# A delta-rule recurrence feeding a SwiGLU layer on one core: the first chunk's chain in another order, and the lower words of the weights added by DMA

## The chip, the cores and the metric

The kernel runs on one core of a Trainium2 chip. The metric is the device time of one execution in microseconds; the kernel before takes 877.96 us (median of 17 runs).

## The reference

Two layers follow each other. The first is a delta-rule recurrence per batch and head, over 768 steps with a 48 x 48 state; the second is a feed-forward layer with an RMS norm in front.

```python
B, H, S, D = (4, 8, 768, 48)
k_n = k / (norm(k, axis=-1) + 1e-06)
for t in range(S):
    y[:, :, t] = einsum('bhd,bhde->bhe', q[:, :, t], state)
    v_old = einsum('bhde,bhd->bhe', state, k_n[:, :, t])
    state = state + beta_t * einsum('bhd,bhe->bhde', k_n[:, :, t], v[:, :, t] - v_old)
x = y as (B*S, H*D)                       # 3072 x 384
xn = x / sqrt(mean(x*x) + 1e-06) * rms_g
out = (silu(xn @ w_gate) * (xn @ w_val)) @ w_out   # d_ff 1536
```

q, k, v and beta arrive as 32-bit floats. The three weight matrices arrive as 64-bit floats and are read as two 32-bit words per number.

## The kernel before

**Chunks and units.** The 768 steps are cut into 6 chunks of 128; a chunk of one batch (8 heads) is a unit. Within a chunk the recurrence is solved as a triangular system: the inverse of a unit triangular matrix of 128 x 128 per head, in blocks of 32 (W). `invert` computes the inverses of the 32 x 32 diagonal blocks of all 32 heads at once on VectorE, with heads and blocks on the partitions: 31 steps of two operations (L440, L449). To get from the layout of the score matrices to that layout, `gather` writes blocks to a DRAM buffer (gd, L359) and reads them back (gblk, L364). The inverses come back the same way: ttb to DRAM (td, L457), then 16 small loads into tt (L468). The same inverses, transposed and multiplied by minus beta (L459), go to DRAM as nd (L473) and come back as ne in 8 loads (L475).

**The chain of a unit** (`recur`): `corner` makes an off-diagonal 32-block of the inverse from two products, p_v with tt (L509) and p_w with ne (L516), copied out by ScalarE (vs, L524; tt, L526). `inner` then forms p_z, p_x and u from the values, `outer` the output p_y and its norm (ScalarE square L718, GpSimd power L727), and `transpose_y` scales y on ScalarE (L731) and transposes it into xt, the input of the feed-forward layer. For the first chunk units 0 and 1 are written out by hand (L637 to L666), the two interleaved with `stay_warm(n)`, which issues n idle matmuls, with `convert(n)`, which issues n steps of the weight conversion, and with `mask_queries`.

**Weights** (`weights`, L230). 18 tiles of 128 x 768 numbers (6 of each half of gate and value, 3 of each half of out: order gate, value, out for the first half, then for the second). A tile is fetched into raw (three buffers, `fetch`, L212), the first three fetches from SP's queue and the others from GpSimd's. ScalarE makes top from the higher word (`shrink`, L225; two buffers); VectorE then takes five steps: shift (L235), sign (L244), exponent part into the weight (L256), times the lower word (L260), plus top (L265). A new fetch follows the fourth step. The top of tile i+1 is issued just before step three of tile i.

**Order.** `begin` writes out the order of everything up to the end of the first inverse: norms of the keys (`normalize`: square on ScalarE L285, sum on VectorE L287, maximum L290 and power L291 on GpSimd, then scaling L294 to L296), their transposes, the key scores, and, during the inverse, queries' transposes and scores. After that a plan of generators with due times sets the order: the feed-forward layer (`ffn`) advances three units per 128 of d_ff, the conversion's remaining steps are due every 0.6 units, and chunks 1 to 5 run beside it. Each engine works through its instructions in that order; where a tile has no free buffer, the instruction that writes it waits for the last reader of an earlier one.

```python
CYC = 3 * FT * B // 2
for i, m in enumerate((0, 1, 0, 1)):
    at(CYC // 4 * i, ffn(m, half_f * (i // 2), half_f * (i // 2 + 1)))
at(0, convert_rest(0.6))
at(1, first)
...
with tc.manual_schedule():
    begin()
    next(first)
    run_plan(60)
run_plan()
```

Of the kernel before, what the change touches and what calls it, by code (L numbers as in the profile page):

```python
# [10 lines left out]
FP32 = mybir.dt.float32  # L11
# [3 lines left out]
ALU = mybir.AluOpType  # L15
# [12 lines left out]
def kernel(  # L28
# [177 lines left out]
    def fetch():  # L206
        i = len(raws)
        if i < len(todo):
            raw = bits.tile([128, WT], I64, name="raw", bufs=3)
            src = todo[i][1]  # L210
            to = raw if len(src.shape) == 2 else raw.rearrange("p (n m) -> p n m", m=DM)
            (nc.sync if i < 3 else nc.gpsimd).dma_start(out=to, in_=src)  # L212
            raws.append(raw)

    def words(raw):
# [14 lines left out]
    def weights():  # L230
        for i, ((dst, src), raw) in enumerate(zip(todo, raws)):
            low, high = words(raw)
            top = tops[i]
            top_u, dst_u = top.bitcast(U32), dst.bitcast(U32)
            nc.vector.tensor_scalar(  # L235
                out=top_u,
                in0=top_u,
                scalar1=3,
                scalar2=0x7FFFFFFF,
                op0=ALU.logical_shift_left,  # L240
                op1=ALU.bitwise_and,
            )
            yield
            nc.vector.scalar_tensor_tensor(  # L244
                out=top_u,
                in0=high,
                scalar=0x80000000,
                in1=top_u,
                op0=ALU.bitwise_and,
                op1=ALU.bitwise_or,  # L250
            )
            yield
            if i + 1 < len(todo):
                tops.append(shrink(raws[i + 1]))

            nc.vector.tensor_scalar(  # L256
                out=dst_u, in0=top_u, scalar1=0xFF800000, scalar2=None, op0=ALU.bitwise_and
            )
            yield
            nc.vector.scalar_tensor_tensor(  # L260
                out=dst, in0=low, scalar=2.0**-52, in1=dst, op0=ALU.mult, op1=ALU.mult
            )
            fetch()
            yield
            nc.vector.tensor_tensor(out=dst, in0=dst, in1=top, op=ALU.add)  # L265
            yield
        bits_pool.close()

# [13 lines left out]
    def normalize(n):  # L282
        kn = kpad[n % NK]
        ksq = work.tile([128, H, D], FP32, name="ksq", bufs=1)
        nc.scalar.square(ksq, kn[:, :, 0:D])  # L285
        ksum = work.tile([128, H], FP32, name="ksum")
        nc.vector.tensor_reduce(out=ksum, in_=ksq, axis=AXL.X, op=ALU.add)  # L287
        knrm = work.tile([128, H], FP32, name="knrm")

        nc.gpsimd.tensor_scalar_max(ksum, ksum, 1e-30)  # L290
        nc.gpsimd.tensor_tensor(out=knrm, in0=ksum, in1=half, op=ALU.pow)  # L291
        yield
        krec = work.tile([128, H], FP32, name="krec")
        nc.vector.tensor_scalar_add(knrm, knrm, 1e-6)  # L294
        nc.vector.reciprocal(krec, knrm)
        (nc.vector if n < B else nc.gpsimd).tensor_tensor(  # L296
            out=kn[:, :, 0:D],
            in0=kn[:, :, 0:D],
            in1=krec[:, :, None].to_broadcast([128, H, D]),
            op=ALU.mult,  # L300
        )
        yield
# [68 lines left out]
    def prepare(n):  # L371
        norm_k = normalize(n)
        next(norm_k)
        yield 1.5
        next(norm_k)
        yield 2.5
        transpose(n, qpad[n % 2], Q0)
        if n + 2 < NU:
            load_q(n + 2)
        yield 3  # L380
        transpose(n, kpad[n % NK], K0)
        yield 2
        score(n, crossed((0, slice(0, 3)), (1, slice(1, 4))), both)
        yield 1
        gather(n)
# [45 lines left out]
    def invert(c, dt):  # L431
        nc.gpsimd.memset(ttb, 0.0)  # L432
        nc.gpsimd.memset(ttb.rearrange("p j i -> p (j i)")[:, 0 : W * W : W + 1], 1.0)
        yield dt
        for i in range(W - 1):
            n = W - 1 - i
            shape = [128, i + 1, n]
            tmp_b = work.tile([128, W * W // 4], FP32, name="tmp")
            tmp = tmp_b[:, 0 : n * (i + 1)].rearrange("p (k j) -> p k j", j=n)
            nc.vector.scalar_tensor_tensor(  # L440
                out=tmp,
                in0=gblk[:, i, None, i + 1 :].to_broadcast(shape),
                scalar=nbeta[:, c, i : i + 1],
                in1=ttb[:, 0 : i + 1, i : i + 1].to_broadcast(shape),
                op0=ALU.mult,
                op1=ALU.mult,
            )
            to = ttb[:, 0 : i + 1, i + 1 :]
            nc.vector.tensor_tensor(out=to, in0=to, in1=tmp, op=ALU.add)  # L449
            if c == 0 and i > W // 2:  # L450
                stay_warm(2, tmp_b[:, 0 : min(128, n * (i + 1))])
            yield dt
        if c == 0:
            stay_warm(20)
        td = dram.tile([128, W, W], FP32, name="td")
        nd = dram.tile([128, W, W], FP32, name="nd")
        nc.sync.dma_start(out=td, in_=ttb)  # L457

        nc.vector.tensor_tensor(  # L459
            out=gblk,  # L460
            in0=ttb.rearrange("p s m -> p m s"),
            in1=nbeta[:, c, :, None].to_broadcast([128, W, W]),
            op=ALU.mult,
        )
        for b in range(B):
            for a in (1, 3, 0, 2):
                o = W * (a % 2)
                nc.sync.dma_start(  # L468
                    out=tt[b][W * a : W * (a + 1), :, o : o + W],
                    in_=td[a * BH + b * H : a * BH + (b + 1) * H].rearrange("h r j -> r h j"),  # L470
                )
            if b == 0:
                nc.sync.dma_start(out=nd, in_=gblk)  # L473
            for a in (0, 2):
                nc.sync.dma_start(  # L475
                    out=ne[W * a : W * (a + 1), b * H : (b + 1) * H],
                    in_=nd[a * BH + b * H : a * BH + (b + 1) * H].rearrange("h r j -> r h j"),
                )
        yield dt
# [13 lines left out]
    def recur(c, dt):  # L493
# [4 lines left out]
            return beta_t[p, c, b * H : (b + 1) * H, None].to_broadcast([HC, H, D])  # L498


        def corner(b_v, b_w):
            p_v = ps_delta([128, H, W], "p_v") if b_v in units else None
            p_w = ps_delta([128, H, W], "p_w") if b_w in units else None
            for h in range(H):
                for a in (0, 2):
                    wa, wb = (slice(W * x, W * (x + 1)) for x in (a, a + 1))
# [7 lines left out]
                        )  # L514
                    if b_w in units:
                        nc.tensor.matmul(  # L516
                            p_w[wa, h], ne[wa, b_w * H + h], vss[b_w][wa, h], skip_group_check=True
                        )
            if b_v in units:
                vss[b_v] = work.tile([128, H, W], FP32, name="vs")  # L520
            for a in (0, 2):
                wa = slice(W * a, W * (a + 1))
                if b_v in units:
                    nc.scalar.copy(vss[b_v][wa], p_v[wa])  # L524
                if b_w in units:
                    nc.scalar.copy(tt[b_w][wa, :, W:HC], p_w[wa])  # L526


        def outer(b_k, b_y):
# [107 lines left out]
        if c == 0:  # L637

            corner(0, None)
            stay_warm(3)  # L640
            convert(1)
            corner(None, 0)
            stay_warm(2)
            corner(1, None)
            inner(None, None, 0)
            convert(1)
            corner(None, 1)
            stay_warm(3)
            inner(0, None, 1)
            stay_warm(4)  # L650
            convert(1)
            inner(1, 0, None)
            stay_warm(4)
            u_0, u_1 = us[0], us[1]
            outer(None, 0)
            mask_queries(1)
            inner(None, 1, None)
            stay_warm(2)
            convert(1)
            outer(None, 1)  # L660
            convert(1)
            transpose_y(0, scale(*ys.pop(0)))
            stay_warm(4)
            convert(2)
            transpose_y(1, scale(*ys.pop(1)))
            convert(4)  # L666
            yield
# [34 lines left out]
        for s in range(-3, B + 2):  # L702
# [1 line left out]
            yield dt  # L704
            outer(s + 1, s - 1)
            yield dt
            corner(s + 3, s + 2)
            if s - 1 in units:
                ys[s - 1] = scale(*ys[s - 1])
            if s - 2 in units:  # L710
# [108 lines left out]
    def begin():  # L819
        setup()  # L820
        stay_warm(14)
        norms = [normalize(n) for n in range(B)]
        for n in range(3):
            next(norms[n])
        next(norms[0])
        transpose(0, kpad[0], K0)
        next(norms[3])
        tops.append(shrink(raws[0]))
        next(norms[1])
        transpose(1, kpad[1], K0)  # L830
        for n in range(B):
            p_gs = score_part(n, K0)
# [7 lines left out]
        for i in range(W):  # L840
# [5 lines left out]
                load_v(n)  # L846
            if what == 3 and n < B:
                keep_queries(n, score_part(n, Q0))
            if i == 6:
                nc.scalar.memzero(tt_all)  # L850
            if i == 12:
# [61 lines left out]
```

## Time and profile before

| what | us |
|---|---|
| median of 17 runs | 877.96 (876.89 to 882.01) |
| profiled execution | 881.04 |
| its span | 879.3 |
| TensorE busy | 826.8 |
| VectorE busy | 409.9 |
| ScalarE busy | 252.5 |
| GpSimd busy | 106.5 |

The profile counts an engine as busy while an instruction runs; matmuls are pipelined, so a busy TensorE is not one at its peak. In the lists that follow, L and a number is the line of the code, a name with an arrow is what is written and read, and what stands in square brackets is the idle time ahead of an instruction and what ended it. DMA issues are shown by the engine whose queue they are on (SPq, ACTq, POOL). Of the span, the first 95 us lie before the first product of the feed-forward layer; from 95 to about 180 the weight conversion runs beside it; the second chunk's inverse ends at 209.5.

### The profile page before, as it was taken

To read this page: it belongs to the slowest core of one execution; us is meant where nothing else is said; L and a number is where in the kernel's file an instruction comes from. 1 tells how busy PE (TensorE), PEld (TensorE's weight loads), DVE (VectorE), ACT (ScalarE), POOL (GpSimd) and SP (SyncE) were. 2 spreads that over 40 slices of the span, in tenths; PEclk is the share of its full clock that TensorE was granted. 3 is DMA by queue.
4 is the path that set the end of the run, shared out by engine and by line. 5 is a ranking of instruction groups with operands and counts; after the bars stand their busy time and mean duration, and the time that the engine had idled before them with its cause. 6 is when DMAs were issued, how large, how long until landed. Compare 5 with 4: busy or idle time off the path is not lost.

```text
span 879.3 us, 19862 instructions
## 1 busy us (share of the span) xinstructions
PE 826.8 (94%) x8438; PEld 645.6 (73%) x8438; DVE 409.9 (47%) x1005; ACT 252.5 (29%) x651; POOL 106.5 (12%) x151
## 2 busy tenths in 40 slices
PE   7377899898999999999999999999999999999998
PEld 6267677576877777787777787777787777777776
DVE  5684878885243392243392333491332491221100
ACT  4512536410334312334312334312234212221101
POOL 4100154300041000131000131000130000000000
PEclk8576999999999999999999999999999999999999
DMA  7715546302232103122203121103121103000000
GB/s 186 168 44 132 146 118 174 100 18 78 46 74 39 46 18 85 39 56 39 46 18 85 39 63 37 42 18 86 39 55 22 37 34 70 2 19 1 18 1 18
DMA packets 150168, 51.82 MB, mean 59 GB/s; under 512 B 142368, under 2 KB 145440, under 8 KB 150080
## 3 DMA queue, kind: packets, MB, share of 16 engines
q1 hardware_dynamic: 126160, 36.13, 17.4%
q0 software_dynamic: 2160, 11.80, 4.2%
q10 hardware_dynamic: 21760, 2.63, 1.9%
q8 instruction: 66, 1.08, 0.5%
q14 instruction: 22, 0.18, 0.1%
HBM read 36.37 MB, written 14.16 MB: 57 GB/s over the span
## 4 chain that ended last, share of the span: by engine, by line
PE 76%; DVE 13%; DMA 2%; issue 2%; ACT 2%; POOL 1%; ACTq 0%; DVEq 0%; SPq 0%; POOLq 0%
PE p_gv L770 36%; PE p_o L757 18%; DVE tmp L440 5%; DVE ttb L449 4%; PE p_g L327 3%; PE p_y L543 2%; PE p_z L599 2%; PE p_t L311 2%; PE p_k L581 2%; PE p_x L617 2%; PE p_y L581 2%; PE p_fill L183 1%; PE p_v L509 1%; DMA gblk<-gd 1%; PE p_z L608 1%
## 5 line engine op out<-in xcount | busy, mean ns | idle before, releaser
L757 PE MATMUL p_o<-wo_sb,h_f 128*128 128x384 f32 x576 | 216.6, 500 | 9.6 <-DVE h_f L781 9.0
L770 PE MATMUL p_gv<-xt,wg_sb 128*128 128x256 f32 x864 | 215.5, 386 | 1.2 <-DVE xt L741 1.2
L770 PE MATMUL p_gv<-xt,wv_sb 128*128 128x256 f32 x864 | 214.6, 384 | 1.0 <-DVE wv_sb L265 1.0
L770 PEld LDWEIGHTS p_gv<-xt,wg_sb 128*128 128x128 f32 x864 | 160.8, 191 | 41.0 <-DVE xt L741 1.5
L770 PEld LDWEIGHTS p_gv<-xt,wv_sb 128*128 128x128 f32 x864 | 161.5, 191 | 25.8 <-issue 2.5
L781 DVE TENSOR_TENSOR h_f<-sil,p_gv 128x256 f32<-128x256 f32 x144 | 60.2, 418 | 237.2 <-ACT sil L779 237.1
L779 ACT ACTIVATE sil<-p_gv 128x256 f32<-128x256 f32 x144 | 55.3, 384 | 342.0 <-PE p_gv L770 324.2
L757 PEld LDWEIGHTS p_o<-wo_sb,h_f 128*128 128x128 f32 x576 | 104.8, 191 | 61.9 <-DVE h_f L781 14.5
L440 DVE SCALAR_TENSOR_TENSOR tmp<-gblk,nbeta,ttb 128x31 f32<-128x31 f32 (+15 forms) x186 | 74.7, 402 | 14.3 <-DMA gblk<-gd 6.9
L449 DVE TENSOR_TENSOR ttb<-ttb,tmp 128x31 f32<-128x31 f32 (+15 forms) x186 | 63.7, 342 | 6.4
L341 DVE TENSOR_TENSOR gp<-p_g,mask 64x128 f32<-64x128 f32 (+1 forms) x160 | 38.7, 310 | 36.6 <-ACT gp L337 32.1
L291 POOL TENSOR_TENSOR knrm<-ksum,half 128x8 f32<-128x8 f32 x24 | 41.6, 1734 | 2.0
L316 ACT COPY kqt<-p_t 128x512 f32<-128x512 f32 x48 | 28.1, 585 | 41.8 <-PE p_t L311 41.2
L726 POOL TENSOR_SCALAR ms<-ms 128x1 f32<-128x1 f32 x24 | 5.8, 241 | 282.2 <-ACT y L718 281.9
L432 POOL MEMSET ttb<- 128x1024 f32 x6 | 5.8, 959 | 238.1 <-DMA td<-ttb 238.1
L599 PEld LDWEIGHTS p_z<-v_raw,tt 64*64 64x64 f32 x768 | 25.7, 140 | 9.5 <-issue 7.5
L327 PE MATMUL p_g<-kqt 64*64 64x192 f32 x640 | 31.7, 331 | 0.3 <-ACT kqt L316 0.3
L617 PE MATMUL p_x<-tt,gp 64*64 64x64 f32 x384 | 29.0, 229 | 0.6 <-ACT tt L526 0.6
L599 PE MATMUL p_z<-v_raw,tt 64*64 64x48 f32 x768 | 28.9, 225 | 0.1
L524 ACT COPY vs<-p_v 32x256 f32<-32x256 f32 x48 | 17.4, 362 | 39.4 <-PE p_w L516 25.2
L327 PEld LDWEIGHTS p_g<-kqt 64*64 64x64 f32 x640 | 23.2, 132 | 7.4 <-issue 5.5
L617 PEld LDWEIGHTS p_x<-tt,gp 64*64 64x64 f32 x384 | 25.6, 142 | 3.3 <-ACT tt L526 2.3
(94 smaller groups left out, 823.5 us busy)
## 6 DMA issues: line engine op xcount, KB each, us to landing
kpad<-in_k_dram SPq DMA_DIRECT2D x24, 192.0 KB, 2.7
qpad<-in_q_dram SPq DMA_DIRECT2D x24, 192.0 KB, 2.8
raw<-in_moe_w_val_dram POOLq DMA_DIRECT2D x6, 768.0 KB, 5.5
v_raw<-in_v_dram SPq DMA_DIRECT2D x24, 192.0 KB, 3.0
raw<-in_moe_w_out_dram POOLq DMA_DIRECT2D x6, 768.0 KB, 4.8
out_dram<-o_sb SPq DMA_DIRECT2D x24, 192.0 KB, 1.9
gblk<-gd SPq DMA_DIRECT2D x6, 512.0 KB, 3.4
td<-ttb SPq DMA_DIRECT2D x6, 512.0 KB, 2.6
```

The costliest lines, as they stand in the source:

```text
L291: nc.gpsimd.tensor_tensor(out=knrm, in0=ksum, in1=half, op=ALU.pow)
L327: nc.tensor.matmul(to, pair[d, K1 if i else K0], pair[d, places], skip_group_check=True)
L341: nc.vector.tensor_tensor(out=to[p, :, place], in0=p_g[p, :, place], in1=mask[p, i, None].to_broadcast([p.stop, 2, HC]), op=ALU.mult,)
L440: nc.vector.scalar_tensor_tensor(out=tmp, in0=gblk[:, i, None, i + 1 :].to_broadcast(shape), scalar=nbeta[:, c, i : i + 1], in1=ttb[:, 0 : ...
L449: nc.vector.tensor_tensor(out=to, in0=to, in1=tmp, op=ALU.add)
L581: nc.tensor.matmul(p_o[p, 2 * j : 2 * j + 2].rearrange("p h d -> p (h d)"), kq[:, j, place], st[:, j], start=(alone or j == 0), stop=alone ...
L599: nc.tensor.matmul(p_zs[b_z][p, h], tt[b_z][p, h], r[p, h], start=(h == 0), stop=(p is lo), skip_group_check=True,)
L617: nc.tensor.matmul(p_x[lo, h], gp[b_x][hi, h, HC * K0 : HC * (K0 + 1)], tt[b_x][hi, h], skip_group_check=True,)
L757: nc.tensor.matmul(p_o[i], h_f[:, i * C : (i + 1) * C], wo_sb[:, f], start=(f == f0), stop=(f == f1 - 1),)
L770: nc.tensor.matmul(p_gv[:, i], w_sb[:, t, f * 128 : (f + 1) * 128], xt[:, t], start=(t == 0), stop=(t == KT - 1),)
L779: nc.scalar.activation(out=sil, in_=p_gv[:, 0], func=ACTF.Silu)
L781: nc.vector.tensor_tensor(out=h_f, in0=sil, in1=p_gv[:, 1], op=ALU.mult)
```

## The change

In the first chunk nd and ne no longer pass through DRAM: `corner` transposes the diagonal blocks of tt with TensorE into a second half of p_w, and VectorE multiplies them by minus beta into ne. Units 0 and 1 go through each stage one after the other. The idle matmuls inside the inverse are gone, and their numbers elsewhere differ. `normalize` yields once more, after the square, and its maximum runs on VectorE; `begin` starts the norms in another order. The fourth and fifth raw tiles are fetched from ScalarE's queue during the first inverse, not after the conversion of the first and second tile. In the conversion, the exponent part goes into top instead of the weight, the sign step writes the weight, and the last step, the sum, is a GpSimd DMA that adds top to the weight. A tile so has four steps for `convert` instead of five.

```diff
@@ -209,7 +209,7 @@
             raw = bits.tile([128, WT], I64, name="raw", bufs=3)
             src = todo[i][1]
             to = raw if len(src.shape) == 2 else raw.rearrange("p (n m) -> p n m", m=DM)
-            (nc.sync if i < 3 else nc.gpsimd).dma_start(out=to, in_=src)
+            (nc.sync if i < 3 else nc.scalar if i < 5 else nc.gpsimd).dma_start(out=to, in_=src)
             raws.append(raw)
     def words(raw):
@@ -242,7 +242,7 @@
             )
             yield
             nc.vector.scalar_tensor_tensor(
-                out=top_u,
+                out=dst_u,
                 in0=high,
                 scalar=0x80000000,
                 in1=top_u,
@@ -254,15 +254,15 @@
                 tops.append(shrink(raws[i + 1]))
             nc.vector.tensor_scalar(
-                out=dst_u, in0=top_u, scalar1=0xFF800000, scalar2=None, op0=ALU.bitwise_and
+                out=top_u, in0=dst_u, scalar1=0xFF800000, scalar2=None, op0=ALU.bitwise_and
             )
             yield
             nc.vector.scalar_tensor_tensor(
-                out=dst, in0=low, scalar=2.0**-52, in1=dst, op0=ALU.mult, op1=ALU.mult
-            )
-            fetch()
-            yield
-            nc.vector.tensor_tensor(out=dst, in0=dst, in1=top, op=ALU.add)
+                out=top, in0=low, scalar=2.0**-52, in1=top, op0=ALU.mult, op1=ALU.mult
+            )
+            if i > 1:
+                fetch()
+            nc.gpsimd.dma_start(out=dst, in_=top, accum_op=ALU.add)
             yield
         bits_pool.close()
@@ -283,11 +283,12 @@
         kn = kpad[n % NK]
         ksq = work.tile([128, H, D], FP32, name="ksq", bufs=1)
         nc.scalar.square(ksq, kn[:, :, 0:D])
+        yield
         ksum = work.tile([128, H], FP32, name="ksum")
         nc.vector.tensor_reduce(out=ksum, in_=ksq, axis=AXL.X, op=ALU.add)
         knrm = work.tile([128, H], FP32, name="knrm")
-        nc.gpsimd.tensor_scalar_max(ksum, ksum, 1e-30)
+        nc.vector.tensor_scalar_max(ksum, ksum, 1e-30)
         nc.gpsimd.tensor_tensor(out=knrm, in0=ksum, in1=half, op=ALU.pow)
         yield
         krec = work.tile([128, H], FP32, name="krec")
@@ -370,6 +371,7 @@
     def prepare(n):
         norm_k = normalize(n)
+        next(norm_k)
         next(norm_k)
         yield 1.5
         next(norm_k)
@@ -447,31 +449,29 @@
             )
             to = ttb[:, 0 : i + 1, i + 1 :]
             nc.vector.tensor_tensor(out=to, in0=to, in1=tmp, op=ALU.add)
-            if c == 0 and i > W // 2:
-                stay_warm(2, tmp_b[:, 0 : min(128, n * (i + 1))])
             yield dt
         if c == 0:
-            stay_warm(20)
+            stay_warm(13, ttb[:, 0:4].rearrange("p k j -> p (k j)"))
         td = dram.tile([128, W, W], FP32, name="td")
-        nd = dram.tile([128, W, W], FP32, name="nd")
         nc.sync.dma_start(out=td, in_=ttb)
-
-        nc.vector.tensor_tensor(
-            out=gblk,
-            in0=ttb.rearrange("p s m -> p m s"),
-            in1=nbeta[:, c, :, None].to_broadcast([128, W, W]),
-            op=ALU.mult,
-        )
+        if c > 0:
+
+            nd = dram.tile([128, W, W], FP32, name="nd")
+            nc.vector.tensor_tensor(
+                out=gblk,
+                in0=ttb.rearrange("p s m -> p m s"),
+                in1=nbeta[:, c, :, None].to_broadcast([128, W, W]),
+                op=ALU.mult,
+            )
+            nc.sync.dma_start(out=nd, in_=gblk)
         for b in range(B):
-            for a in (1, 3, 0, 2):
+            for a in range(NBLK):
                 o = W * (a % 2)
                 nc.sync.dma_start(
                     out=tt[b][W * a : W * (a + 1), :, o : o + W],
                     in_=td[a * BH + b * H : a * BH + (b + 1) * H].rearrange("h r j -> r h j"),
                 )
-            if b == 0:
-                nc.sync.dma_start(out=nd, in_=gblk)
-            for a in (0, 2):
+            for a in (0, 2) if c > 0 else ():
                 nc.sync.dma_start(
                     out=ne[W * a : W * (a + 1), b * H : (b + 1) * H],
                     in_=nd[a * BH + b * H : a * BH + (b + 1) * H].rearrange("h r j -> r h j"),
@@ -498,9 +498,10 @@
             return beta_t[p, c, b * H : (b + 1) * H, None].to_broadcast([HC, H, D])
+
         def corner(b_v, b_w):
             p_v = ps_delta([128, H, W], "p_v") if b_v in units else None
-            p_w = ps_delta([128, H, W], "p_w") if b_w in units else None
+            p_w = ps_delta([128, 2, H, W], "p_w")
             for h in range(H):
                 for a in (0, 2):
                     wa, wb = (slice(W * x, W * (x + 1)) for x in (a, a + 1))
@@ -514,16 +515,38 @@
                         )
                     if b_w in units:
                         nc.tensor.matmul(
-                            p_w[wa, h], ne[wa, b_w * H + h], vss[b_w][wa, h], skip_group_check=True
+                            p_w[wa, 0, h],
+                            ne[wa, b_w * H + h],
+                            vss[b_w][wa, h],
+                            skip_group_check=True,
                         )
+                for a in range(NBLK if b_v in units and c == 0 else 0):
+                    wa = slice(W * a, W * (a + 1))
+                    o = W * (a % 2)
+                    nc.tensor.matmul(
+                        p_w[wa, 1, h],
+                        tt[b_v][wa, h, o : o + W],
+                        ident[wa, wa],
+                        skip_group_check=True,
+                    )
             if b_v in units:
                 vss[b_v] = work.tile([128, H, W], FP32, name="vs")
+                if c == 0:
+                    own = slice(b_v * H, (b_v + 1) * H)
+                    nc.vector.scalar_tensor_tensor(
+                        out=ne[:, own],
+                        in0=p_w[:, 1],
+                        scalar=-1.0,
+                        in1=beta_t[:, c, own, None].to_broadcast([128, H, W]),
+                        op0=ALU.mult,
+                        op1=ALU.mult,
+                    )
             for a in (0, 2):
                 wa = slice(W * a, W * (a + 1))
                 if b_v in units:
                     nc.scalar.copy(vss[b_v][wa], p_v[wa])
                 if b_w in units:
-                    nc.scalar.copy(tt[b_w][wa, :, W:HC], p_w[wa])
+                    nc.scalar.copy(tt[b_w][wa, :, W:HC], p_w[wa, 0])
         def outer(b_k, b_y):
@@ -637,31 +660,29 @@
         if c == 0:
             corner(0, None)
-            stay_warm(3)
+            corner(1, None)
             convert(1)
+            stay_warm(2)
             corner(None, 0)
+            corner(None, 1)
+            convert(2)
             stay_warm(2)
-            corner(1, None)
-            inner(None, None, 0)
+            inner(0, None, 0)
+            inner(1, None, 1)
+            stay_warm(1)
+            inner(None, 0, None)
+            inner(None, 1, None)
+            mask_queries(1)
             convert(1)
-            corner(None, 1)
-            stay_warm(3)
-            inner(0, None, 1)
-            stay_warm(4)
+            u_0, u_1 = us[0], us[1]
+            stay_warm(2)
+            outer(None, 0)
+            outer(None, 1)
+            convert(3)
+            stay_warm(5)
+            transpose_y(0, scale(*ys.pop(0)))
             convert(1)
-            inner(1, 0, None)
-            stay_warm(4)
-            u_0, u_1 = us[0], us[1]
-            outer(None, 0)
-            mask_queries(1)
-            inner(None, 1, None)
             stay_warm(2)
-            convert(1)
-            outer(None, 1)
-            convert(1)
-            transpose_y(0, scale(*ys.pop(0)))
-            stay_warm(4)
-            convert(2)
             transpose_y(1, scale(*ys.pop(1)))
             convert(4)
             yield
@@ -704,7 +725,8 @@
             yield dt
             outer(s + 1, s - 1)
             yield dt
-            corner(s + 3, s + 2)
+            if s + 2 in units or s + 3 in units:
+                corner(s + 3, s + 2)
             if s - 1 in units:
                 ys[s - 1] = scale(*ys[s - 1])
             if s - 2 in units:
@@ -820,13 +842,12 @@
         setup()
         stay_warm(14)
         norms = [normalize(n) for n in range(B)]
-        for n in range(3):
+        for n in (0, 0, 1, 1, 2, 2, 3, 0):
             next(norms[n])
-        next(norms[0])
         transpose(0, kpad[0], K0)
-        next(norms[3])
         tops.append(shrink(raws[0]))
-        next(norms[1])
+        for n in (3, 1):
+            next(norms[n])
         transpose(1, kpad[1], K0)
         for n in range(B):
             p_gs = score_part(n, K0)
@@ -846,6 +867,8 @@
                 load_v(n)
             if what == 3 and n < B:
                 keep_queries(n, score_part(n, Q0))
+                if n < 2:
+                    fetch()
             if i == 6:
                 nc.scalar.memzero(tt_all)
             if i == 12:
```

## The prediction

> **What bounds the kernel now.** I read the busy times by stretch first, then the chain that ended last up to 100 us, then each engine's timeline there, then the DMA issues with their landing times.
>
> ```profile
> 0.00:95.00 95.00, 63.30 (x788) 54.80 (x788) 61.46 (x136) 32.85 (x67) 15.30 (x27) 0.73 0.50 124
> 95.00:155.00 60.00, 56.11 (x628) 42.71 (x628) 50.31 (x91) 30.12 (x71) 23.34 (x25) 1.00 0.58 158
> 155.00:215.00 60.00, 51.66 (x240) 37.76 (x240) 50.75 (x117) 13.32 (x35) 7.09 (x9) 0.91 0.20 61
> 215.00:879.30 664.30, 655.77 (x6784) 510.33 (x6782) 247.38 (x663) 176.25 (x479) 60.80 (x91) 1.00 0.18 40
> ```
> Columns: stretch and length; busy PE, PEld, DVE, ACT, POOL; clock; DMA share; GB/s. After 215 us TensorE is busy 655.77 of 664.30, so what the change moves before 215 us shifts the end one for one. TensorE idles 31.7 us in the first 95, 3.9 in the next 60, 8.3 in the next. From 95 to 215 VectorE is 84% busy and runs level with TensorE.
>
> ```profile
> 28.20 6.07 DMA gblk<-gd
> 66.36 2.68 DMA nd<-gblk
> 69.05 3.95 DMA ne<-nd
> 73.13 1.20 PE p_w L516 x32
> ```
> The chain: start, length, work. The key blocks' return from DRAM starts the 32-step inverse at 34.4 us; after it the negated blocks go to DRAM and back until 73.0 before TensorE may form p_w.
>
> ```profile
> 21.88 0.79 POOL L212 DMA_DIRECT2D raw<-in_moe_w_val_dram  x1 [8.53 <-DVE wg_sb L260]
> 26.52 0.55 POOL L212 DMA_DIRECT2D raw<-in_moe_w_val_dram  x1 [3.85 <-issue]
> ...
> 67.78 0.92 ACT L225 ACTIVATE top<-raw 128x768 f32<-128x768 f32 x1 [8.95 <-DVE wg_sb L265]
> 68.61 0.73 ACT L524 COPY vs<-p_v 32x256 f32<-32x256 f32 x2
> ...
> 63.63 0.55 DVE L235 TENSOR_SCALAR top<-top 128x768 uint32<-128x768 uint32 x1
> 64.21 0.96 DVE L244 SCALAR_TENSOR_TENSOR top<-raw,top 128x768 uint32<-128x768 uint32 x1
> 65.21 0.56 DVE L256 TENSOR_SCALAR wg_sb<-top 128x768 uint32<-128x768 uint32 x1
> 65.80 0.96 DVE L260 SCALAR_TENSOR_TENSOR wg_sb<-raw,wg_sb 128x768 f32<-128x768 uint32 x1
> 66.79 0.96 DVE L265 TENSOR_TENSOR wg_sb<-wg_sb,top 128x768 f32<-128x768 f32 x1
> ...
> 98.83 0.70 PE L770 MATMUL p_gv<-xt,wv_sb 128*128 128x256 f32 x2 [1.02 <-DVE wv_sb L265]
> 177.29 2.59 PE L757 MATMUL p_o<-wo_sb,h_f 128*128 128x384 f32 x4 [2.29 <-DVE h_f L781]
> ```
> Timelines. Two raw tiles are fetched just as the blocks go through DRAM. One weight tile is five VectorE passes, 3.99 us. The ScalarE pass L225 already waits for the last pass on an earlier tile (only two tops exist), and in ScalarE's order it stands ahead of the copy of vs that the chain needs. TensorE's first value product waits for the sixth weight.
>
> ```profile
> raw<-in_moe_w_val_dram POOLq DMA_DIRECT2D x6, 768.0 KB, 5.5
> ...
> DMA to landing us min/median/max: 4.4/5.1/6.8
> ```
> Fetches (KB each, issue to landing); the second line is over all 18.
>
> **The Trainium skill.** "DMA: Bandwidth & Descriptors", section on SWDGE, HWDGE and iDMA: an accumulating DMA can be issued by GpSimd alone, and GpSimd has one queue context. All software traffic here is indeed on q0, so an add waits behind the fetch issued just ahead of it. Same page, anatomy of one DMA: about 2.0 us fixed plus bytes/436e3, the semaphore firing only after the last byte is confirmed. That gives 3.8 us for a 768 KB fetch (trace: 4.4 to 6.8) and 2.9 us for a plain 384 KB one. "TensorE: Matmul & The Clock Gate", Part 1: an idle array falls to half clock. The trace agrees (0.50 from 72 to 84 us).
>
> **The change part by part**, against the profiled execution (span 879.3, its own time 881.04). I put the difference on the median of the runs, 877.96, which lies 3.1 lower.
>
> *Front.* The third square and sum come before the first scaling, and the maximum moves from GpSimd (0.25) to VectorE (0.16, by the L294 row). In before, the fourth square sits behind a copy until 9.38, so unit 1 is scaled at 10.9 although its power ended at 8.75. Now its scaling can start at about 9.3: **-1.4**. Before the last key copy VectorE does a 0.55 pass in place of the 0.96 add: **-0.4**. The fetches of tiles 4 and 5 move from 21.9 and 26.5 to ScalarE's queue behind the query copies (28 us and later), so the blocks travel almost alone: in before the last gather issue ends at 24.7 and they are back at 34.3, 9.6 us. The medians for these transfers are 1.9 and 3.4, 5.3 in all. Two adds of 384 KB now run beside them, so I take 5.9: **-3.7** (bounds -4.3 and 0). The inverse loses its fills, which held VectorE: steps 0 to 14 took 12.65, the equally large 16 to 30 took 13.70: **-1.2** with the waits on fills. The inverse ends near 55.1 instead of 61.8. I call this end T.
>
> *Chain after the inverse.* Gone: the 1.94 us multiply, nd, and eight ne loads with their SP issues. Added per unit: 32 small transposes (at most 1.2, the p_w row) and one 128x256 VectorE operation (about 0.5), beside copies. Taken alone, stage by stage in turn, this would bring the first p_gv from T+33.6 to about T+23.
>
> But the fifth pass is now a DMA, and its landing takes the place of the add as what frees top. Let L be the time from the end of the multiply to the landing. The trace has no accumulating DMA. Below: with nothing ahead, 0.7 issue plus 2.9 by the page, 3.6. Above: a fetch ahead (5.1) plus an add that moves bytes at a third of the fetch's rate (some 4), 10. Taken: fetch ahead, its bytes done 4.2 us after its issue (the one issued at 72.8 filled the DMA rate until about 77 and landed at 4.7), two reads and a write at half a fetch's rate per byte 1.8, and again 0.5 to the landing: **L = 6.5**. VectorE: the multiply of tile 3 ends at T+1.55, its add lands at T+8.1, ScalarE makes the top of tile 5 by 9.0. Tile 4's multiply ends at T+6.15, its add lands near 12.7, and only then may ScalarE make the next top (13.6) and copy vs, which the transposes had ready by about T+8. So p_w starts at T+14.4 (before: T+11.4). Stages, from the rows of before: p_w and copies to 17.5, inner products to 20, second ones to 22.5, mask to 24.6 and outer products to 25.7. Tile 6's multiply ends at 26.1 and lands at 32.6. The top of tile 8 waits for that on ScalarE, ahead of the scaling of the second y: first p_gv at T+35.2. Tile 7 goes the same way (43) and holds the first silu: p_o starts at T+44.5 against T+43.1 before. **+1.4**; this part hands back all that the shorter chain wins.
>
> *Under the FFN* (tiles 8 to 18). A tile took (179.69-98.79)/12 = 6.74 us; four of five steps, 5.4. The step spacing in the plan is unchanged, so VectorE's load per plan unit barely falls. With two tops, two tiles take at least L + 0.9 (ScalarE) + 5.0 (four passes, 3.03, with the other work between). GpSimd is 39% busy with powers and scalings ahead of its DMA issues, so I take L = 7.9 here: 6.9 per tile, +1.5 on the eight tiles with a fetch ahead: **+12**. ScalarE's stall also stands before silu and the copies of scores. Bounds: 0 at L under 5, +24 at 11. The conversion ends some ten plan units earlier, which removes waits like that at 177 us: **-2.7** (all waits of p_o for h_f but the one in the second inverse). The maximum on VectorE in later chunks (20 times 0.16) is covered by TensorE.
>
> Sum: -1.4 -0.4 -3.7 -1.2 +1.4 +12 -2.7 = **+4.0**, so 885.0 in the profiled execution's terms and **882.0** for the median.
>
> **Rivals.** (1) *The add lands quickly*, L = 5, and 5.6 under the FFN: p_o at T+40 (-3.1), 5.75 per tile (+3); in all -9.5, **868.5**. For it: VectorE loses 18 passes, 17 us, where it is 84% busy, and DMA share is only 0.58. Against: the fetch ahead in the one queue takes 4.4 at its best. It decides the sign from L below about 6. (2) *The adding units are slow* or descriptors are held up by VectorE, L = 10, and 11 under the FFN: p_o 12 later, +24; in all +27, **905**. For it: an add reads two streams. Against: 384 KB is half a fetch. (3) *Everything cancels*: the plan's slack swallows a third of the stalls (TensorE has the next p_gv, 3 us, to go on with), +8 in place of +12: **878**. That the change does not do what it says: the adds are certain, but the front's -3.7 may not come, since the adds cross the same window; then +7.7, inside the forecast's range.
>
> **How the numbers follow.** Forecast 0.54, its own range 879 to 895; rival 1 0.32, rival 2 0.07, rival 3 0.07. About 0.2% (1.8 us) is what a measurement of this kernel can tell from no change. The first four terms are near-certain gains of several us, the stall is near-certain too, and only its size is open, so both signs hold much: 866 to 899 takes in most of rival 1 and leaves out the slow end. Faster 0.32, same 0.07, slower 0.61.
>
> **What would show it.** The inverse should start near 29 us and take 26; tt loads follow with no nd. In ScalarE's timeline, each top should wait for an accumulating DMA on wg_sb, wv_sb or wo_sb, with vs(0) at about T+14 and the first p_gv near T+35. Landings of the adds should read 5.5 to 7.5 us. If they read under 4, or top never waits, the forecast is wrong and rival 1 holds; if the inverse starts after 33, the front was wrong.

## The result, and the profile after

The changed kernel takes 922.55 us (median of 8 runs) against 878.19 (47 runs of the kernel before beside it): a ratio of 1.0502, interval 1.0487 to 1.0518, 44 us slower. The time lies above the range that was given; the direction was the forecast's. The profiled execution has a span of 920.6 us against 879.3.

Busy time by stretch, of the kernel after (stretch and length; PE, PEld, DVE, ACT, POOL with instructions; clock; DMA share; GB/s):

```profile
0.00:95.00 95.00, 51.07 (x827) 43.71 (x827) 59.36 (x141) 32.65 (x66) 20.44 (x28) 0.66 0.63 151
95.00:155.00 60.00, 38.89 (x552) 29.07 (x553) 26.93 (x44) 14.23 (x29) 13.67 (x16) 0.73 0.57 129
155.00:215.00 60.00, 45.08 (x294) 32.66 (x296) 27.55 (x68) 22.83 (x58) 21.67 (x21) 0.84 0.58 125
215.00:260.00 45.00, 42.00 (x208) 31.48 (x198) 30.79 (x83) 7.40 (x22) 1.11 (x2) 1.00 0.18 54
```

From 95 to 215 us TensorE was busy 107.8 us before and is busy 84.0 now; VectorE fell from 101.1 to 54.5, ScalarE from 43.4 to 37.1. All the engines stand still for part of the time. The DMA share is no higher than before in the first of the two stretches (0.57 against 0.58); in the second it is (0.58 against 0.20), since the conversion lasts longer. So no engine is overloaded: something is waited for.

ScalarE's timeline after (start, length, instruction, and in brackets the idle time ahead of it and what ended it):

```profile
72.46 0.89 ACT L225 ACTIVATE top<-raw 128x768 f32<-128x768 f32 x1 [4.70 <-DMA wv_sb<-top]
73.26 0.73 ACT L547 COPY vs<-p_v 32x256 f32<-32x256 f32 x2
...
98.24 0.89 ACT L225 ACTIVATE top<-raw 128x768 f32<-128x768 f32 x1 [8.39 <-DMA wv_sb<-top]
99.03 0.57 ACT L753 ACTIVATE y<-p_y,rs 128x384 f32<-128x384 f32 x1
109.12 0.91 ACT L225 ACTIVATE top<-raw 128x768 f32<-128x768 f32 x1 [9.53 <-DMA wo_sb<-top]
...
115.41 0.89 ACT L225 ACTIVATE top<-raw 128x768 f32<-128x768 f32 x1 [4.84 <-DMA wo_sb<-top]
116.32 1.28 ACT L801 ACT_TABLE_LOAD   x1
117.61 0.38 ACT L801 ACTIVATE sil<-p_gv 128x256 f32<-128x256 f32 x1
```

Each top waits for the DMA that adds an earlier top to its weight. Right behind it stands what the chain needs: first vs, then the scaling of the second y, then the first silu. Before, vs was copied at 68.61, and the first silu came at 103.07.

VectorE and TensorE after, same columns:

```profile
61.90 0.96 DVE L260 SCALAR_TENSOR_TENSOR top<-raw,top 128x768 f32<-128x768 uint32 x1
...
87.77 0.96 DVE L260 SCALAR_TENSOR_TENSOR top<-raw,top 128x768 f32<-128x768 uint32 x1
...
104.10 0.96 DVE L260 SCALAR_TENSOR_TENSOR top<-raw,top 128x768 f32<-128x768 uint32 x1
...
118.03 0.42 DVE L803 TENSOR_TENSOR h_f<-sil,p_gv 128x256 f32<-128x256 f32 x1 [4.52 <-ACT sil L801]
118.37 0.95 DVE L260 SCALAR_TENSOR_TENSOR top<-raw,top 128x768 f32<-128x768 uint32 x1
```

```profile
101.20 2.93 PE L792 MATMUL p_gv<-xt,wg_sb 128*128 128x256 f32 x6 [0.65 <-DVE xt L763]
118.51 2.93 PE L779 MATMUL p_o<-wo_sb,h_f 128*128 128x384 f32 x4 [6.88 <-DVE h_f L803]
```

The same two products before:

```profile
95.39 1.56 PE L770 MATMUL p_gv<-xt,wg_sb 128*128 128x256 f32 x6 [1.23 <-DVE xt L741]
104.83 1.56 PE L757 MATMUL p_o<-wo_sb,h_f 128*128 128x384 f32 x4 [0.49 <-DVE wo_sb L265]
```

Reading VectorE's and ScalarE's timelines together gives the time from the end of a multiply (L260) to the release of its buffer: 62.86 to 72.46, 88.73 to 98.24, 105.06 to 115.41, that is 9.5 to 10.4 us. Over all thirteen adds that have a fetch issued ahead of them, the time from the multiply's end to the landing is 7.1 to 15.5 us, 9.2 in the median. The first product of the feed-forward layer starts 5.8 us later than before and the first p_o 13.7 later; p_o also runs at half clock (2.93 us for what took 1.56).

The add's own line, all 18 (issue to landing):

```profile
DMA to landing us min/median/max: 4.1/6.8/9.1
```

The five adds without a fetch ahead land in 4.1 to 5.0 us, the thirteen behind one in 6.2 to 9.1.

### The profile page after: what moved, and what is told of

It is laid out like the page before. It is cut to its first block, busy times and chain, and to the rows that moved or that the text cites. A ratio compares the mean times of both kernels' runs of the same rounds, so it can differ in the third digit from the quotient of the medians.

```text
span 920.6 us, 20200 instructions
## 1 busy us (share of the span) xinstructions
PE 830.8 (90%) x8608; PEld 643.6 (70%) x8608; DVE 394.1 (43%) x1014; ACT 253.3 (28%) x651; POOL 113.3 (12%) x143
## 4 chain that ended last, share of the span: by engine, by line
PE 69%; DVE 9%; DMA 6%; ACT 2%; issue 1%; POOL 1%; ACTq 0%; SPq 0%; POOLq 0%; DVEq 0%
PE p_gv L792 34%; PE p_o L779 17%; DVE tmp L442 4%; DVE ttb L451 3%; PE p_g L328 3%; DMA wo_sb<-top 2%; PE p_y L566 2%; PE p_k L604 2%; PE p_z L622 2%; PE p_t L312 2%; PE p_y L604 2%; DMA wg_sb<-top 1%; PE p_x L640 1%; PE p_v L510 1%; PE p_w L517 1%
## 5 line engine op out<-in xcount | busy, mean ns | idle before, releaser
L792 PE MATMUL p_gv<-xt,wv_sb 128*128 128x256 f32 x864 | 219.1, 390 | 0.0
L792 PE MATMUL p_gv<-xt,wg_sb 128*128 128x256 f32 x864 | 217.7, 388 | 0.7 <-DVE xt L763 0.7
L792 PEld LDWEIGHTS p_gv<-xt,wv_sb 128*128 128x128 f32 x864 | 163.9, 194 | 25.3 <-issue 2.5
L292 POOL TENSOR_TENSOR knrm<-ksum,half 128x8 f32<-128x8 f32 x24 | 43.1, 1797 | 65.7 <-DVE ksum L291 65.7
L225 ACT ACTIVATE top<-raw 128x768 f32<-128x768 f32 x18 | 16.2, 900 | 97.0 <-issue 25.8
L510 PEld LDWEIGHTS p_v<-tt,gp 32*32 32x32 f32 x768 | 18.2, 110 | 21.5 <-issue 14.8
L566 PE MATMUL p_y<-u,gp 128*64 128x48 f32 x768 | 27.2, 225 | 3.7 <-DVE u L647 3.5
```

Of the source, the lines that this page charges most:

```text
L566: nc.tensor.matmul(p_y[p, h], gp[b_y][:, h, HC * place : HC * (place + 1)], u[:, h], start=(c == 0 and h == 0), stop=True, skip_group_chec ...
L792: nc.tensor.matmul(p_gv[:, i], w_sb[:, t, f * 128 : (f + 1) * 128], xt[:, t], start=(t == 0), stop=(t == KT - 1),)
```

## The experiments

Three theories stood against each other. W: the loss is ScalarE waiting, in its order, for adds to land. T: the adds cost by their traffic and their place in GpSimd's queue, whoever waits. F: the first-chunk edits lose. All ratios are to the kernel before, run beside each.

**chunk_only**: the last two steps of the conversion as before, all else as changed.

```diff
-            nc.gpsimd.dma_start(out=dst, in_=top, accum_op=ALU.add)
+            yield
+            nc.vector.tensor_tensor(out=dst, in0=dst, in1=top, op=ALU.add)
```

> The first-chunk edits with the five VectorE passes of before. Theory W (ScalarE's next top waits in order for an accumulating DMA to land): the first-chunk edits gain by themselves, about 866 us, first p_gv near 84 us. Rival F (the first-chunk edits lose, by a cold TensorE and by adding work to VectorE): above 890 us. Rival T (the adds' traffic and queue cost, whoever waits): also about 866.

878.4 us, ratio 0.9989 (0.9969 to 1.0009). None of the three expectations holds: the first-chunk edits bring no gain and no loss that can be told. Its first p_gv starts at 90.18, 5.2 us earlier than before, and its first p_o is 5.1 us earlier, but its second p_o is 2.5 us later (114.09 against 111.59). One place shows in TensorE's timeline of this kernel, in the middle of one burst of small matmuls:

```profile
102.28 0.19 PE L518 MATMUL p_w<-vs,ne 32*32 32x32 f32 x1
106.22 0.26 PE L527 MATMUL p_w<-ident,tt 32*32 32x32 f32 x7 [3.75 <-issue]
```

```profile
107.00:112.00 5.00, 5.00 (x55) 3.97 (x54) 2.82 (x4) 2.05 (x6) 0.00 (x0) 0.52 0.15 61
```

"issue" means that TensorE waited for nothing that the profile shows. L527 are the new transposes. From 107 to 112 us, after the stop, the clock is 0.52 (the third last number of the stretch), where the kernel before had 1.00.

**conv_only**: the kernel before with the changed conversion alone (the four steps and the add by DMA).

> The kernel before with only the conversion changed: four passes and an accumulating DMA. W and T: it carries the whole loss, 915 to 930 us. F: under 895 us.

919.38 us, ratio 1.0492 (1.0457 to 1.0526). The conversion alone gives 41 of the 44 us, so F falls as the cause of the loss. In its trace the wait reaches TensorE directly:

```profile
84.45 1.45 PE L515 MATMUL p_w<-vs,ne 32*32 32x32 f32 x32 [11.91 <-ACT vs L523]
```

In the kernel before, the same p_w waited 4.5 us, for the load of ne.

**top_in_weight**: ScalarE writes top into the weight's place, VectorE's first two passes work there, and only the product needs one of the two buffers.

```diff
-        top = bits.tile([128, WT], FP32, name="top", bufs=2)
+        top = todo[len(tops)][0]
...
+            top = bits.tile([128, WT], FP32, name="top", bufs=2)
             nc.vector.tensor_scalar(
-                out=top_u, in0=dst_u, scalar1=0xFF800000, scalar2=None, op0=ALU.bitwise_and
+                out=top.bitcast(U32), in0=dst_u, scalar1=0xFF800000, scalar2=None, op0=ALU.bitwise_and
             )
```

> The changed kernel, with ScalarE writing the top into the weight's own place and the two buffers used only for the product that the DMA adds: the same passes, fetches and adds, but ScalarE no longer waits for a buffer; VectorE's third pass waits for the add two tiles back instead. W: most of the loss is gone, 860 to 872 us. T: the adds' traffic and GpSimd's queue are unchanged, so above 905 us.

888.08 us, ratio 1.0126 (1.0092 to 1.016). It lies between the two expectations, much nearer to W's: with every add still there, 34 of the 44 us are gone. Who waits for adds, in the kernel after and then in this one (us in total, times, longest):

```profile
ACT top L225 <- DMA wo_sb<-top: 25.0, 4, 9.5
ACT top L225 <- DMA wv_sb<-top: 22.7, 4, 8.4
ACT top L225 <- DMA wg_sb<-top: 20.8, 3, 9.1
```

```profile
DVE top L254 <- DMA wv_sb<-top: 5.1, 3, 3.1
DVE top L254 <- DMA wo_sb<-top: 3.2, 3, 2.1
PE p_gv L790 <- DMA wv_sb<-top: 2.9, 1, 2.9
DVE top L254 <- DMA wg_sb<-top: 2.7, 1, 2.7
```

68.5 us of waiting on ScalarE have become 11.0 on VectorE and 2.9 on TensorE. The edit lifts every wait of ScalarE for a buffer, also those for VectorE to be done with one; no run tells the two apart.

**add_first**: the add is issued ahead of the fetch.

```diff
-            if i > 1:
-                fetch()
             nc.gpsimd.dma_start(out=dst, in_=top, accum_op=ALU.add)
+            if i > 1:
+                fetch()
```

> The changed kernel with each add issued ahead of the fetch instead of behind it. W: an add lands 4.5 to 5 us after the multiply, not 9.5, so the eight tiles under the FFN and the chain lose about half as much: 885 to 900 us. T: the same bytes, 918 to 926 us.

896.02 us, ratio 1.0231 (1.0193 to 1.027): W's number. The add's line in this kernel:

```profile
DMA to landing us min/median/max: 3.9/4.3/7.4
```

The order of two issues on one queue takes the median landing from 6.8 to 4.3 us, and 26 us off the kernel. Counted from the end of the multiply, the median of the same thirteen tiles goes from 9.2 to 5.8 us.

**half_transposes**: chunk_only, with only the two diagonal blocks transposed that p_w reads.

```diff
-                for a in range(NBLK if b_v in units and c == 0 else 0):
+                for a in (0, 2) if b_v in units and c == 0 else ():
```

(and the multiply into ne on these two groups of partitions).

> The first-chunk edits with the five VectorE passes, and only the two diagonal blocks per unit that p_w uses transposed (16 small matmuls per unit, not 32). Theory B (TensorE stops 2 to 4 us inside each long burst of small matmuls with no recorded wait, because of the burst's length): the stops shrink or go, 870 to 875 us. Rival (the first-chunk edits' gain is lost elsewhere, to a cold clock and late loads): 876 to 880 us, with stops as before.

874.93 us, ratio 0.9966 (0.9949 to 0.9984): faster than both kernels, by 3 us against before. Its interval overlaps that of chunk_only, so the halving itself is not told apart by time. The stops are: TensorE's waits of this kernel from 56 to 120 us hold no "issue" of p_w.

```profile
PE p_v L511 <- DMA tt<-td: 4.0, 1, 4.0
PE p_x L643 <- ACT tt L552: 2.4, 1, 2.4
PE p_xt L765 <- ACT y L756: 0.9, 2, 0.7
```

In chunk_only the same list has

```profile
PE p_w L527 <- issue: 6.4, 2, 3.7
```

**in_weight_add_first**: top_in_weight with the order of add_first.

> Top made in the weight's own place and each add issued ahead of the fetch. W: nothing waits long for an add any more, so the time falls to that of the first-chunk edits alone, 876 to 881 us. T (the adds' traffic and GpSimd's queue cost by themselves): stays at 886 to 890 us.

889.06 us, ratio 1.0108 (1.0069 to 1.0147). W's expectation fails and T's holds: no engine's list of waits names an add any more, and some 10 us remain over chunk_only. In this kernel a fetch of an out tile takes 7.5 us to land in the median (before 4.8, kernel after 5.8).

**plain_copy**: the changed kernel without `accum_op`.

> The changed kernel with a plain copy of top over the weight in place of the add (it leaves the sum out): the same bytes written, one stream read less. If the adding itself is slow, copies land at least 2 us sooner and the time falls to about 905 us; if the price is the place in the queue behind the fetch and the fixed cost, they land within 1 us of the adds and the time stays at 915 to 925 us.

905.11 us, ratio 1.0303 (1.0263 to 1.0343). The copies land at

```profile
DMA to landing us min/median/max: 2.6/5.6/8.0
```

1.2 us sooner than the adds in the median and 1.5 in the least. Neither half of the expectation holds as written: the time falls to about 905 us, as the first half said, but the landing by less than 2 us. The 17 us are not all the landing's: the run also reads one stream less, and in the two profiled executions its first inverse starts 3.5 us earlier. How they divide is not shown.

**idle_store**: half_transposes with a store of each finished tile that nobody waits for.

```diff
+            copy = dram.tile([128, WT], FP32, name=f"copy{i}", bufs=1)
+            nc.gpsimd.dma_start(out=copy, in_=dst)
```

> The half_transposes kernel with one DMA more per weight tile: GpSimd stores the finished tile, 384 KB, to a DRAM buffer that nobody reads or waits for. If the adds' traffic and queue place cost by themselves (T), this costs 6 to 12 us against half_transposes: 881 to 887 us. If only waiting costs (W), it stays at 873 to 877 us.

881.84 us, ratio 1.0042 (1.0025 to 1.006), 7 us more than half_transposes. So T holds as a second, smaller cause: a DMA of 384 KB per tile costs about that much with nobody behind it. What else moves lands later. Loads from 56 to 215 us (KB each, issue to landing), half_transposes and then idle_store:

```profile
kpad<-in_k_dram SPq DMA_DIRECT2D x4, 192.0 KB, 3.2
v_raw<-in_v_dram SPq DMA_DIRECT2D x4, 192.0 KB, 3.7
```

```profile
kpad<-in_k_dram SPq DMA_DIRECT2D x4, 192.0 KB, 6.7
v_raw<-in_v_dram SPq DMA_DIRECT2D x4, 192.0 KB, 6.9
```

But in the profiled executions these loads are not where the time goes. idle_store is 13.3 us longer there. Its first p_gv is 13.3 us later (96.44 against 83.11), and from there to the end both take 787.2 us. 8.4 of the 13.3 us are there at the first step of the inverse, in half_transposes and then in idle_store:

```profile
28.15 0.25 DVE L443 SCALAR_TENSOR_TENSOR tmp<-gblk,nbeta,ttb 128x31 f32<-128x31 f32 x1 [3.66 <-DMA gblk<-gd]
```

```profile
36.56 0.25 DVE L445 SCALAR_TENSOR_TENSOR tmp<-gblk,nbeta,ttb 128x31 f32<-128x31 f32 x1 [13.27 <-DMA gblk<-gd]
```

Two of the stores are issued while the gather's blocks pass through DRAM. There the 32 KB writes to gd land in 3.0 us in the median against 1.6. Beside the feed-forward layer the stores cost nothing that shows. This is one execution of each kernel, and chunk_only, without stores, starts its inverse at 31.82; so how much of the later start the stores cause is not shown.

**half_in_weight_add_first**: in_weight_add_first with half the transposes.

> The in_weight_add_first kernel with half the transposes: DMA adds that nobody waits for long, and no stops in the bursts. If the 18 VectorE passes saved are worth something, below 872 us; if the traffic takes it back (T), 880 to 887 us; if neither matters, 875 us.

881.43 us, ratio 1.0034 (1.0022 to 1.0045). Eighteen VectorE passes fewer buy nothing in sum: against half_transposes, which has them, it is 6.5 us slower, as much as idle_store. In the profiled executions the part from the first p_gv on is 2.5 us shorter (784.7 against 787.2), and the part ahead of it 8.8 us longer. A stop of 2.6 us in p_w is back here, and one of 3.4 in idle_store, although the bursts are short in both, while in_weight_add_first, with the long ones, shows none; so the length of the burst does not decide it.

**half_after**: the changed kernel with half the transposes.

> The changed kernel with half the transposes and nothing else. B: the stops in the bursts, 2.7 us here, go, and the chain still waits for the adds: 915 to 922 us. If the bursts carried a large share of the loss: under 912 us.

923.88 us, ratio 1.0498 (1.0465 to 1.0532), as the changed kernel and just above B's range, and TensorE's stops in p_w are gone. Their going changes nothing that can be told there, as is to be expected where the chain waits for ScalarE anyway.

## Why the prediction was right and where it was wrong

**The mechanism held, the sizes did not.** The forecast said that the add's landing takes the place of VectorE's sum as what frees top, and that ScalarE waits for it in order ahead of vs, of the scaling of the second y and of the first silu. All three show at those places. Three terms of the sum failed. L, the time from the multiply's end to the landing, was taken as 6.5 and 7.9 us and measured 9.2 in the median. The four passes "with the other work between" were taken as 5.0 us and took some 9. And what does not hang on L was counted as a gain, 6.7 us at the front and in the inverse; the runs show no gain of the first-chunk edits that lasts (chunk_only), and a loss of 7 to 10 us from adds or stores for which nobody waits long (idle_store, in_weight_add_first), which the sum puts at nothing under the FFN and in the chain.

**The front** was forecast at -5.5 and gave -3.1 in this pair of executions (the inverse starts at 31.29, before 34.41). VectorE's last key copy starts at 19.00 where it started at 22.14, more than the -1.8 of norms and order. But the gather's issues last until 23.68 (before: 24.71), and the blocks take 7.6 us from there to the first step of the inverse where 5.9 were assumed. Two adds, issued at 18.9 and 22.5, cross this stretch, but that they are the cause is not shown: chunk_only, which has none, starts its inverse at 31.82. Over the kernels with the same edits to the front it starts between 27.75 and 36.56, so one execution of each does not size this term.

**The inverse** takes 25.65 us, before 27.33: -1.7 against -1.2. It ends at 56.9, not 55.1.

**The chain**, +1.4 in the forecast, gave +18.5 from the inverse's end to the first p_o (61.6 against 43.1 us). Here L was mis-sized: 6.5 us taken, 7.1 to 10.2 measured for tiles 3 to 8. The waits that end at 98.24 and 115.41 follow one another with the chain behind both. The wait that ends at 72.46 does not count in full, since TensorE is held just as long by something else, the tt blocks of unit 1:

```profile
72.49 0.31 PE L510 MATMUL p_v<-tt,gp 32*32 32x32 f32 x2 [3.84 <-DMA tt<-td]
75.65 2.25 PE L517 MATMUL p_w<-vs,ne 32*32 32x32 f32 x64
```

So p_w starts 18.7 us after the inverse, not 14.4. In top_in_weight, where ScalarE waits for no add, it is 18.9; in half_transposes and chunk_only, which have no adds, 13.2 and 15.8. The forecast had the transposes ready 8 us after the inverse and did not count late blocks. Besides, TensorE is at half clock after its waits: the first p_gv takes 2.93 us, after 8.76 us of waiting for y, and the one at 107.02 takes 1.56.

**Under the FFN**, +12 in the forecast; after the first p_o another 28 us are lost by the end. From the top at 109.12 to that at 189.86 eight tiles take 10.1 us each, not 6.9. L was taken as 7.9, and these eight adds took 10.2 on average. The landing itself was foreseen, 5.5 to 7.5 us (median 6.8). What came out larger is the time from the multiply to the issue of the add, for which the forecast had put 1.4 us on top of the chain's L: it is mostly 1.1 to 1.3 us, with a fetch to issue first, but 5.8 and 8.6 us on two tiles. The first of the two, on VectorE, ScalarE and GpSimd in turn:

```profile
145.63 0.91 DVE L260 SCALAR_TENSOR_TENSOR top<-raw,top 128x768 f32<-128x768 uint32 x1
...
148.54 0.89 ACT L225 ACTIVATE top<-raw 128x768 f32<-128x768 f32 x1 [8.34 <-DMA wg_sb<-top]
149.33 0.48 ACT L740 ACTIVATE y<-p_y 128x384 f32<-128x384 f32 x1
...
149.99 0.22 POOL L748 TENSOR_SCALAR ms<-ms 128x1 f32<-128x1 f32 x1 [4.72 <-ACT y L740]
...
151.73 0.65 POOL L212 DMA_DIRECT2D raw<-in_moe_w_val_dram  x1
152.37 1.09 POOL L265 DMA_DIRECT2D wg_sb<-top  x1
```

GpSimd, in its own order, stands at ms, which needs ScalarE's y; y stands behind a top that waits for the add before. So on these two tiles a late add also delays the issue of the next one.

With 10.2 for L, the forecast's formula for two tiles (20.2 us) leaves some 9 us for the four passes and what lies between, where 5.0 were taken. The wait sits ahead of silu; without silu there is no h_f, VectorE holds at h_f with the next passes behind it (118.03 and 118.37 above), and TensorE holds at p_o. The work that was to hide the wait is queued behind it and comes afterwards.

The price of a microsecond of L was about right: 3.4 us less (add_first) are worth 26 us of the kernel, nearly eight to one, where the sum had about seven. But for the 5.8 us of add_first the sum gives some 871 us, an estimate between its forecast and its quick-add rival, and 896 were measured. Two measured amounts come near these 25 us: the first-chunk edits, of which 12 us more were expected than chunk_only shows, and the 10 us that remain in in_weight_add_first.

**The rivals.** The slow-add rival, 905 us, had about the right L (10 to 11) and was still 17 us short, for want of the same part. The quick-add rival was wrong in its premise: the fetch ahead in the same queue holds the add, as add_first shows.

**The account.** 922.55 to 888.08: 34 us, gone with ScalarE's waits for a buffer. 888.08 to 878.4: 10 us that stay while the adds are there and ScalarE does not wait for them; idle_store finds some 7 for DMAs of that size with nobody waiting, in its profiled execution all ahead of the first p_gv. The first-chunk edits: nothing that can be told. Why their 5 us are lost again is only partly shown: one stop and a cold array in TensorE are seen there, and what causes the stops stays open. A third buffer for top, the plainest cure, was not tried.

## What to carry to other kernels

Before a pass is moved from an engine to a DMA, look at what its end releases: with two buffers and work in strict order, the landing time (here 4 to 9 us) replaces a pass of 0.96 us, and everything queued behind the instruction that waits stops with it, including the work that was to cover the wait. Count the landing from the end of the work that it follows, with the transfers queued ahead of it and with whatever the issuing engine itself has to wait for first. Issuing the short, awaited DMA before the long, unawaited one needed no instruction more and took 26 us off here. If the DMA must stay, let the scarce buffer be taken as late as possible, by the engine that can best wait.

## What was not expected of the hardware

- An adding DMA of 384 KB within on-chip memory landed in 3.9 us (add_first) and 4.1 us (kernel after) at best and a plain copy of the same size in 2.6, so the adding cost about 1.5 us.
- Eighteen DMAs of 384 KB for which nothing waits cost 7 us. 192 KB loads beside them landed in 6.7 and 6.9 us in place of 3.2 and 3.7, but the time was lost earlier, ahead of the first p_gv (all of the 13.3 us in the one profiled execution of each kernel).
- TensorE stopped for about 2 to 4 us inside bursts of small matmuls with no recorded wait. With half the transposes the stops went in two kernels and were there, once each, in two others; one kernel with all the transposes (in_weight_add_first) had none. The cause is open.
